# An attention and mixture-of-experts kernel on one core: embeddings loaded first, two more filler products, the first batch's W2 split moved into eight steps in a row

## The chip, the cores and the metric

One core of a Trainium2 chip (trn2) runs the whole program. Times are device microseconds (us) of one execution. The kernel before was timed in three runs.

## What is computed

A compressed attention turns its output into tokens; every token then goes to one of eight experts. Cut to what matters:

```python
# batch 8, heads 8, seq 576, head_dim 64, 32 memory slots
a = softmax(phi over seq)                      # 576 x 32 per head
k_m, v_m = a.T @ k, a.T @ v                    # 32 x 64 per head
attn = softmax(q @ k_m.T / 8) ; o = attn @ v_m # 576 x 64 per head
x = o as (4608 tokens, 512)                    # heads side by side
en = expert_emb / norm(expert_emb)
logits = x/norm(x) @ en.T / tau                # 4608 x 8
e = argmax(logits); gate = softmax(logits)[e]
out = gate * (relu(x @ w1[e]) @ w2[e])         # w1 512x1024, w2 1024x512
```

## The kernel before

Every engine runs its instructions in the order in which the program writes them; waits between engines and transfers are semaphores. Transfers start on three queues: SyncE's (SP), ScalarE's (ACT) and GpSimd's (POOL).

**The head.** The first batch's `phi` comes in two halves on SP's queue, then its keys and values in four tiles `kx0` to `kx3`, then `q`. ACT's queue carries the last 64 rows of keys and values (`kl`), the expert embeddings (`emb`, into part of `sT`) and `tau`. ACT takes the exponential of the first half of `phi` (`softmax`), then the square sum of the embeddings (`router`, the line with `AF.Square`), then the exponential of the second half. TensorE (PE) transposes the exponentials in three groups (`turn`, tiles `te`), with filler products on a constant between them (`warm`, tile `hot`), and multiplies them with the keys and values, tile by tile (`slots`, tiles `acc0t` and `acc0m`, the order of tiles is 0, 1, tail, 2, 3). The next batch's `phi`, keys and values are loaded behind these, and its transposes and `slots` run in the head as well.

**A batch.** `project` and `first` make h = relu(x W1) in 16 steps of six products (tile `ph`, four PSUM buffers in rotation). After each step ACT writes the rounded `hh` (and, from step 8 on, `h4`), and VectorE (DVE) the remainder `hl`; a buffer is free when both have read it. `second` multiplies by W2 (tile `py`, out of the same rotation): first the last 64 tokens, straight from `w2s`, then the others from the rounded `wh` and the remainder `wl`.

**The split of W2.** `split_w` makes `wh` and `wl` of one eighth of W2: a cast `wh<-w2s` (for the first batch on ACT, later on POOL) and a subtract `wl<-w2s,wh` on POOL.

**The steps.** `steps` hangs other work behind the steps of `first` and `second`. For the first batch, the norms and gates of its tokens (`late`, of `root`, `sqrt` and `gates`: small DVE instructions of 128x5 and 128x40 on SBUF tiles) are spread behind steps 3 to 8 of `first`; behind step 8 comes ACT's exponential `l` (in `gates`), which needs DVE's subtract in the line before it. Behind steps 9 and 11 stand the copies of the next batch's scores.

Of the kernel before, what the change touches and what calls it, by code (L numbers as in the profile page):

```python
# [21 lines left out]
N, DM, E, FF = B * S, H * D, 8, 1024  # L22
# [208 lines left out]
class Kernel:  # L231
# [60 lines left out]
    def consts(self):  # L292
# [9 lines left out]
        nc.vector.tensor_scalar(out=self.eb, in0=self.i8, scalar1=1.0 / (E * P), scalar2=None, op0=ALU.mult)  # L302
        nc.vector.memset(self.vv, 0.0)

    def load_router(self):
        nc, st = self.nc, self.st.tile
        self.em, self.hq = (self.sT[:E, 1, :DM], self.w2s[:E, 7])
        nc.scalar.dma_start(self.em, self.emb)
        self.tv = st([E, 1], F32, name="tv")
        nc.scalar.dma_start(self.tv, self.tau.broadcast_to((E, 1)))  # L310
        nc.scalar.activation(st([P, 1], F32, name="e8"), self.ones[:, :1], AF.Exp)
# [378 lines left out]
    def steps(self, b, t, u):  # L690


        first, second = ([[] for _ in range(n)] for n in (16, 40))

        for j in range(8):
            copy = self.nc.gpsimd.tensor_copy if b else None
            at = first[j if b else 9 + j * 2] if b or j < 4 else second[j - 4]
            at.append(lambda copy=copy: self.split_w(copy))
        if not b:
            late = t.late()  # L700
            first[2].append(lambda: t.attend(3, 4))
            first[3].append(lambda: t.norm(3, 4))
            first[4] += [t.total, lambda: self.load_kv(2)]

            for f in range(3, 9):
                first[f].append(lambda: next(late))
            first[12] += [lambda: self.keep(0), lambda: self.load_q(2)]
        if u:
            c, o = b + 1, 0 if b else 3
            if not b:  # L710
                first[9].append(lambda: self.scores(c))
            for k in range(2):
                first[(3 + k if b else 9 + 2 * k)].append(lambda k=k: self.results(c, k))

            places = (first[6], first[8], first[10], first[12]), (first[12], first[14], second[0], second[3])
            if not b:
                places = (second[3], second[3], second[3], second[7]), (second[7], second[7], second[7], second[10])
            all = slice(0, BL)
            for g in range(NG):
                work = u.weigh((g,), all)  # L720
                places[g][0].append(lambda g=g: u.fill((g,), all, [self.sT[:, i] for i in range(NG)]))
                for at in places[g][1:]:
                    at.append(lambda work=work: next(work, None))
            for at, g in zip((second[0], second[3]) if b else (second[7], second[10]), range(NG)):
                at.append(lambda g=g: (u.divide((g,), all), u.lay(g), u.turn((g,), all)))
            o = 0 if b else 7
            second[17 + o].append(lambda: u.attend(0, 1, pt=self.mm))
            second[19 + o].append(lambda: u.attend(2, 3))
            second[21 + o].append(lambda: u.attend(4))
            second[22 + o] += [lambda: self.load_w2(u.choose()), self.parts, lambda: self.keep(c)]  # L730
            second[23 + o] += [u.owner, u.flags]
            for n, i in enumerate(((0, 1), (2, 3), (4,)) if b else ((2, 3), (4,), (0, 1))):
                second[24 + n + o].append(lambda i=i: u.norm(*i))
            after = u.late()
            for n in (27, 28, 29, 30, 31, 32):
                second[n + o].append(lambda: next(after))
            second[32 + o].append(lambda: list(after))
            m = b + 2
            if m < B:
                for g in range(NG):  # L740
                    second[11 + 3 * g + o].append(lambda g=g: self.softmax(m, (g,)))
                second[18 + o].append(lambda: self.shares(m))
                second[(28 if b else 25) + o].append(lambda: [self.turn(m, i, min(i + 4, 9)) for i in (0, 4, 8)])
                at = second[(31 if b else 28) + o]
                at += [lambda: self.slots(m), lambda: self.blocks(m, 0), lambda: self.blocks(m, 1, True)]
                for g in range(NG):
                    second[(35 + 2 * g if b else 31 + g) + o].append(lambda g=g: self.flip(m, g))
        return first, second
# [152 lines left out]
@with_exitstack  # L901
def moe_linformer(ctx, tc, phiT, qT, kv, kvt, emb, tau, w1, w2, out):
    k = Kernel(ctx, tc, phiT, qT, kv, kvt, emb, tau, w1, w2, out)
    ctx.enter_context(tc.manual_schedule(engines={ET.PE, ET.DVE, ET.Activation, ET.SP, ET.Pool}))


    k.eights()
    k.warm(11)
    k.load_phi(0)
    k.load_kv(0)  # L910
    k.load_q(0)
    k.load_router()
    k.consts()
    accs = [k.ps.tile([P, 4, 2 * D], F32, tag=f"{n}3", name=f"acc0{n}", bufs=1) for n in "tm"]
    for acc in accs:
        k.nc.vector.memset(acc, 0.0)
    router = k.router()
    for g in range(NG):
        k.largest(0, g)
        k.softmax(0, (g,))  # L920
        next(router)
    for i in (0, 4, 8):
        k.turn(0, i, min(i + 4, 9))
        if i < 8:
            k.warm(2)
    k.shares(0)
    k.load_phi(1)
    t = Tokens(k, 0, k.pt)
    keys, values = slice(0, 1), slice(1, 2)
    for ks in ((0, 1), (4,), (2,), (3,)):  # L930
        k.slots(0, accs, ks=ks, first=0 in ks, last=3 in ks)
        if ks[0] < 3:
            k.warm(1)
    k.block(0, 0)
    k.load_kv(1)
    k.flip(0, 0, keys)
    k.block(0, 1, which=(0,))
    k.flip(0, 1, keys)
    first, others = slice(0, 4), slice(4, BL)
    ts = [k.mm([P, P], f"ts0_{g}", 1 + g) for g in range(NG)]  # L940
    k.score(0, ts, 0, P)
    t.fill(range(NG), first, ts)
    k.block(0, 1, which=(1,))
    next(router, None)
    k.flip(0, 0, values)
    k.flip(0, 1, values)
    ts = [k.mm([P, S - P], f"tr0_{g}", g) for g in range(NG)]
    k.score(0, ts, P, S)
    k.squares(0, [k.pt([P, D + E], f"tl0_{g}") for g in range(NG)])
    list(t.weigh(range(NG), first))  # L950
    k.products(0)
    k.warm(5, 2)
    t.divide(range(NG), first)
    t.turn(range(NG), first)
    k.largest(1, 0)
    k.softmax(1, (0,))
    t.attend(0, pt=lambda shape, name: k.mm(shape, name, 2), turned=False)
    e = t.choose((0,))
    k.largest(1, 1)
    k.softmax(1, (1,))  # L960
    k.load_q(1, (0,))
    t.turned(0)
    for i in (0, 4, 8):
        k.turn(1, i, min(i + 4, 9))
        k.turns += not i
        if not i:
            k.warm(8, hot=t.spare)
    t.fill(range(NG), others, ts)
    weights = [t.weigh((g,), others) for g in range(NG)]
    for g in range(NG):  # L970
        next(weights[g])
    for g in range(NG):
        next(weights[g])
        list(weights[g])
    t.owner()
    k.shares(1, v=k.nc.gpsimd)
    k.slots(1, accs)
    k.block(1, 0, alone=True)
    k.tags = 4
    for g in range(NG):  # L980
        k.part(g, slice(0, P), k.nc.scalar.copy)
    k.block(1, 1, alone=True)
    k.flip(1, 0)
    t.divide(range(NG), others)
    t.turn(range(NG), others)
    for g in range(NG):
        k.part(g, slice(P, HS), k.nc.scalar.copy)
    t.norm(0)
    k.load_q(1, (1,))
    k.load_w2(e)  # L990
    k.load_phi(2)
    k.warm(3)
    for b in range(B):
        u = Tokens(k, b + 1, k.pt) if b < B - 1 else None
        left = k.batch(b, t, u)
        t = u
    k.rest(*left)
# [29 lines left out]
```

## Time and profile before

| | before |
|---|---|
| median of 3 runs | 418.95 us (418.62 to 420.69) |
| profiled execution | 421.38 us |
| its span, first to last instruction | 419.0 us |
| PE busy | 97% of the span |
| DVE, ACT, POOL busy | 63%, 41%, 40% |
| mean granted PE clock | 0.992 |

The profiled execution is one execution with its own time, 2.4 us over its span and 2.4 us over the median of the timed runs. Stretches below are counted from the start of its span. "Line" is a line of the program; "released by" in brackets is what ended the idle time before an instruction.

### The profile page before, as it was taken

The page shows a single profiled execution, that of the slowest core. Times are in us where ns is not written, and L with a number is a line of the kernel's source. Part 1 is how long each engine was busy: PE and PEld are TensorE (multiplying, and loading weights), DVE is VectorE, ACT ScalarE, POOL GpSimd, SP SyncE. Part 2 cuts the span into 40 slices and gives each one's busy share as a digit, 9 for nine tenths or more (in the row PEclk, how much of TensorE's full clock was granted, in tenths as well). Part 3 has the DMA queues.
Part 4 walks back from the last instruction along what each step waited for, and adds up shares of the span by engine and source line. Part 5 has one row for each costly group of instructions (what it writes and reads, how often), then busy time and mean ns, then how long its engine had stood idle before and what let it go on. Part 6 is the DMA issues. An engine that isn't in the chain of part 4 may idle for free. (4 is left out here: it accounts for less than half of the span.)

```text
span 419.0 us, 9431 instructions
## 1 busy us (share of the span) xinstructions
PE 405.8 (97%) x3489; PEld 329.5 (79%) x3489; DVE 262.4 (63%) x839; ACT 173.2 (41%) x476; POOL 168.6 (40%) x196
## 2 busy tenths in 40 slices
PE   6989999999999999999999999999999999999993
PEld 2458878788877978879787988879788888879783
DVE  4597796679664795648772695648955495745000
ACT  4466742375225722356313642357223661145110
POOL 0032380387132942259130960339331681359000
PEclk9899999999999999999999999999999999999998
DMA  8979926896769824995469926798349404690101
GB/s 272 345 281 344 362 85 156 283 371 268 154 214 398 334 50 118 344 372 218 75 206 378 364 89 148 241 386 318 60 127 366 155 0 96 201 398 10 37 36 47
DMA packets 69858, 91.19 MB, mean 218 GB/s; under 512 B 41800, under 2 KB 47688, under 8 KB 69808
## 3 DMA queue, kind: packets, MB, share of 16 engines
q1 hardware_dynamic: 66928, 82.00, 59.3%
q0 software_dynamic: 2688, 8.26, 5.3%
q8 instruction: 29, 0.48, 0.5%
q10 hardware_dynamic: 192, 0.28, 0.3%
q14 instruction: 21, 0.17, 0.1%
HBM read 71.19 MB, written 19.33 MB: 216 GB/s over the span
## 5 line engine op out<-in xcount | busy, mean ns | idle before, releaser
L628 PE MATMUL ph<-aT,gh 128*128 128x288 f32 x512 | 103.2, 297 | 0.5 <-DVE gl L612 0.5
L681 PE MATMUL py<-wh,hh 128*128 128x512 f32 x248 | 102.3, 413 | 0.0
L681 PE MATMUL py<-wl,hh 128*128 128x512 f32 x248 | 97.0, 391 | 0.3 <-POOL wl L599 0.3
L681 PE MATMUL py<-wh,hl 128*128 128x512 f32 x248 | 97.1, 392 | 0.0
L599 POOL TENSOR_TENSOR wl<-w2s,wh 128x512 fp32r<-128x512 f32 x64 | 83.4, 1306 | 16.8 <-ACT wh L598 12.3
L628 PEld LDWEIGHTS ph<-aT,gh 128*128 128x128 f32 x512 | 81.7, 188 | 3.0 <-DVE gl L612 1.4
L628 PE MATMUL ph<-aT,gl 128*128 128x288 f32 x256 | 75.4, 294 | 0.0
L634 DVE SCALAR_TENSOR_TENSOR hl<-ph,hh 128x288 fp32r<-128x288 f32 x128 | 56.0, 449 | 22.6 <-ACT hh L631 16.6
L631 ACT ACTIVATE hh<-ph 128x288 fp32r<-128x288 f32 x128 | 52.4, 417 | 32.9 <-PE ph L628 32.3
L686 ACT ACTIVATE ys<-py,gate 128x512 f32<-128x512 f32 (+1 forms) x39 | 25.0, 641 | 96.0 <-issue 48.3
L789 POOL DMA_DIRECT2D out_dram<-ys x28 | 15.5, 553 | 118.2 <-ACT ys L686 110.5
L681 PEld LDWEIGHTS py<-wh,hh 128*128 128x128 f32 x248 | 46.6, 188 | 12.0 <-issue 3.9
L681 PEld LDWEIGHTS py<-wh,hl 128*128 128x128 f32 x248 | 46.5, 188 | 10.2
L681 PEld LDWEIGHTS py<-wl,hh 128*128 128x128 f32 x248 | 46.7, 188 | 8.5 <-POOL wl L599 0.7
L628 PEld LDWEIGHTS ph<-aT,gl 128*128 128x128 f32 x256 | 48.0, 188 | 0.0
L589 POOL TENSOR_TENSOR aT<-aw,aT 128x576 fp32r<-128x576 f32 (+3 forms) x20 | 24.5, 1240 | 43.9 <-PE py L681 33.8
L612 DVE TENSOR_TENSOR gl<-pg,gh 128x512 fp32r<-128x512 f32 x32 | 20.0, 683 | 34.9 <-ACT gh L611 34.9
L598 POOL CAST wh<-w2s 128x512 fp32r<-128x512 f32 x56 | 37.5, 669 | 0.6 <-DMA w2s<-w 0.6
L670 PE MATMUL py<-w2s,h 128*64 128x256 f32 x256 | 29.4, 382 | 0.0
L427 ACT ACTIVATE ex<-ex,nm 128x576 f32<-128x576 f32 x16 | 12.3, 770 | 30.9 <-DVE nm L412 29.9
L670 PEld LDWEIGHTS py<-w2s,h 128*64 128x64 f32 x256 | 17.7, 137 | 9.4 <-DVE hl L634 1.1
L119 DVE TENSOR_REDUCE lg<-po 128x8 f32<-128x16 f32 x40 | 6.8, 173 | 28.1 <-PE po L114 28.0
(168 smaller groups left out, 522.6 us busy)
## 6 DMA issues: line engine op xcount, KB each, us to landing
kx<-kv SPq DMA_DIRECT2D x32, 512.0 KB, 7.0
w2s<-w SPq DMA_DIRECT2D x32, 512.0 KB, 10.2
w1s<-w SPq DMA_DIRECT2D x28, 512.0 KB, 6.5
out_dram<-ys POOLq DMA_DIRECT2D x28, 256.0 KB, 6.0
qt<-qT SPq DMA_DIRECT2D x12, 576.0 KB, 8.4
ad<-aw SPq DMA_DIRECT2D x8, 576.0 KB, 13.0
td<-x SPq DMA_DIRECT2D x56, 72.0 KB, 2.2
ea<-td SPq DMA_DIRECT2D x7, 512.0 KB, 4.1
```

The source lines that it names most:

```text
L427: nc.scalar.activation(x, x, AF.Exp, bias=nm[:, g : g + 1], accum_out=sm[:, g : g + 1])
L589: self.nc.gpsimd.tensor_tensor(out=al, in0=a, in1=ah.bitcast(F32), op=ALU.subtract)
L598: (copy or self.nc.scalar.copy)(h, x)
L599: self.nc.gpsimd.tensor_tensor(out=l, in0=x, in1=h.bitcast(F32), op=ALU.subtract)
L612: nc.vector.tensor_tensor(out=self.gl[:, g, f], in0=ps[g], in1=self.gh[:, g, f].bitcast(F32), op=ALU.subtract)
L628: nc.tensor.matmul(p, lhsT=w[:, g, fs], rhs=x[:, g, to], start=g == 0 and k == 0, stop=g == 1 and k == 2)
L631: nc.scalar.activation(self.hh[:, f, to], p, AF.Relu)
L634: nc.vector.scalar_tensor_tensor(out=self.hl[:, f, to], in0=p, scalar=0.0, in1=self.hh[:, f, to].bitcast(F32), op0=ALU.max, op1=ALU.subtract)
L670: nc.tensor.matmul(p[64 * j : 64 * j + 64], lhsT=self.h4[:, f], rhs=self.w2s[:, f, d * j : d * j + d], start=f == 0, stop=f == 7,)
L681: nc.tensor.matmul(p, lhsT=h[:, f, to], rhs=w[:, f], start=f == 0 and k == 0, stop=f == 7 and k == 2)
L686: nc.scalar.activation(y[:, :d], p, AF.Copy, scale=gate[:, i : i + 1])
L789: eng.dma_start(self.out[r : r + P], y)
```

## The change

Three things change. The load of the embeddings becomes a function of its own and is called ahead of the load of `kl`, so it is first on ACT's queue. The filler products between the first two groups of transposes are four where they were two. The first batch's eight splits, which stood behind steps 9, 11, 13 and 15 of `first` and steps 0 to 3 of `second`, stand behind steps 6 to 13 of `first`, one for each.

```diff
+    def load_emb(self):
+        self.em, self.hq = (self.sT[:E, 1, :DM], self.w2s[:E, 7])
+        self.nc.scalar.dma_start(self.em, self.emb)
+
     def load_router(self):
         nc, st = self.nc, self.st.tile
-        self.em, self.hq = (self.sT[:E, 1, :DM], self.w2s[:E, 7])
-        nc.scalar.dma_start(self.em, self.emb)
...
         for j in range(8):
             copy = self.nc.gpsimd.tensor_copy if b else None
-            at = first[j if b else 9 + j * 2] if b or j < 4 else second[j - 4]
-            at.append(lambda copy=copy: self.split_w(copy))
+            first[j if b else 6 + j].append(lambda copy=copy: self.split_w(copy))
...
     k.load_phi(0)
+    k.load_emb()
     k.load_kv(0)
...
     for i in (0, 4, 8):
         k.turn(0, i, min(i + 4, 9))
         if i < 8:
-            k.warm(2)
+            k.warm(2 if i else 4)
```

ACT's order behind steps 6 to 9 of `first`, batch 0 (`ph_06`, `ph_07`, `ph_10` and `ph_11` are the steps 6 to 9; the line numbers after `_` only count tiles). Before:

```order
L631 ACTIVATE hh<-ph_06_660 128x288
L631 ACTIVATE hh<-ph_07_674 128x288
L631 ACTIVATE hh<-ph_10_687 128x288
L633 ACTIVATE h_96<-ph_10_687 128x64
L213 ACTIVATE l_683<-l_683 128x40
L631 ACTIVATE hh<-ph_11_706 128x288
L633 ACTIVATE h_96<-ph_11_706 128x64
L598 CAST wh<-w2s 128x512
```

and with the change:

```order
L633 ACTIVATE hh<-ph_06_662 128x288
L600 CAST wh<-w2s 128x512
L633 ACTIVATE hh<-ph_07_678 128x288
L600 CAST wh<-w2s 128x512
L633 ACTIVATE hh<-ph_10_693 128x288
L635 ACTIVATE h_96<-ph_10_693 128x64
L600 CAST wh<-w2s 128x512
L213 ACTIVATE l_689<-l_689 128x40
L633 ACTIVATE hh<-ph_11_714 128x288
L635 ACTIVATE h_96<-ph_11_714 128x64
L600 CAST wh<-w2s 128x512
```

Three casts stand ahead of the exponential `l` where there was none; the fourth stands where the first stood.

DVE's order in the same place is the same in both programs; so it reads with the change, from the remainder of step 5 to that of step 8:

```order
L636 SCALAR_TENSOR_TENSOR hl<-ph_05_650,hh 128x288
L42 RECIPROCAL nrr<-nrg 128x5
L43 SCALAR_TENSOR_TENSOR nrr<-nrr,ss_208 128x5
L44 SCALAR_TENSOR_TENSOR nrg<-nrg,nrr 128x5
L636 SCALAR_TENSOR_TENSOR hl<-ph_06_662,hh 128x288
L42 RECIPROCAL nrr<-nrg 128x5
L43 SCALAR_TENSOR_TENSOR nrr<-nrr,ss_208 128x5
L44 SCALAR_TENSOR_TENSOR n_618<-nrg,nrr 128x5
L196 TENSOR_SCALAR n_618<-n_618 128x5
L197 RECIPROCAL n_618<-n_618 128x5
L636 SCALAR_TENSOR_TENSOR hl<-ph_07_678,hh 128x288
L209 TENSOR_TENSOR m_209<-m_209,n_618 128x5
```

Nothing moved here; what moved is POOL's work beside it, since each subtract `wl` follows its cast.

## Rows read from the trace of the kernel before

**Rows 1.** The page's first part: busy us, share of the span, instructions.

```profile
PE 405.8 (97%) x3489; PEld 329.5 (79%) x3489; DVE 262.4 (63%) x839; ACT 173.2 (41%) x476; POOL 168.6 (40%) x196
```

**Rows 2.** Waits of PE over the whole span: us, times, longest.

```profile
PE te L449 <- ACT ex L427: 2.2, 1, 2.2
...
PE py L681 <- POOL wl L599: 0.3, 1, 0.3
```

**Rows 3.** Timeline of the head: start, us, engine, line, tiles, idle before and releaser.

```profile
6.00 0.75 DVE L412 TENSOR_REDUCE nm<-ex 128x1 f32<-128x576 f32 x1 [1.06 <-DMA ex<-phiT]
...
6.44 0.59 PE L351 MATMUL hot<-ones 128*128 128x512 bf16 x2
...
7.73 0.63 ACT L319 ACTIVATE w2s<-sT 8x512 f32<-8x512 f32 x1 [1.90 <-DMA sT<-emb]
...
8.36 0.76 ACT L427 ACTIVATE ex<-ex,nm 128x576 f32<-128x576 f32 x1
...
9.26 1.12 PE L449 MATMUL te<-ident,ex 128*128 128x128 f32 x4 [2.23 <-ACT ex L427]
...
14.54 0.43 PE L469 MATMUL acc0t<-kx,eT 128*32 128x128 f32 x8
```

**Rows 4.** Busy time by stretch; PEclk is the granted clock, then DMA share, GB/s.

```profile
11.00:12.00 1.00, 1.00 (x14) 0.59 (x16) 0.95 (x6) 0.27 (x2) 0.00 (x0) 0.50 1.13 338
```

**Rows 5.** SP's own timeline: the issue of the first batch's last tile, `kx3`.

```profile
5.28 0.61 SPq L375 DMA_DIRECT2D kx<-kv  x1
```

**Rows 6.** DMA issues of that moment and of ACT's `kl`: KB, us to landing.

```profile
kx<-kv SPq DMA_DIRECT2D x1, 512.0 KB, 6.7
...
kl<-kvt ACTq DMA_DIRECT2D x2, 128.0 KB, 4.9
```

**Rows 7.** Busy time by stretch as in Rows 4, from 20 to 25 us.

```profile
20.00:22.00 2.00, 1.04 (x7) 0.65 (x6) 1.84 (x7) 0.61 (x2) 0.00 (x0) 1.00 1.03 404
...
23.20:24.00 0.80, 0.80 (x6) 0.34 (x5) 0.80 (x3) 0.59 (x1) 0.00 (x0) 1.00 0.05 20
24.00:25.00 1.00, 1.00 (x6) 0.43 (x5) 1.00 (x3) 0.97 (x4) 0.49 (x3) 1.00 0.00 0
```

**Rows 8.** PE's timeline: the last 12 of 32 products of the next batch's `acc0t`.

```profile
26.00 0.51 PE L469 MATMUL acc0t<-kx,eT 128*32 128x128 f32 x12
```

**Rows 9.** DVE's timeline, 53 to 61 us.

```profile
53.74 1.72 DVE L72 TENSOR_TENSOR x<-x,mx 128x576 f32<-128x576 f32 x1
...
60.01 0.76 DVE L84 TENSOR_TENSOR x<-x,z 128x576 f32<-128x576 f32 x1
```

**Rows 10.** One line, POOL's subtract, 40 to 60 us: ns minimum, median, maximum.

```profile
L599 POOL TENSOR_TENSOR wl<-w2s,wh x8: 1285/1292/1826, 46.6 to 57.8; 128x512 fp32r<-128x512 f32 x8
```

**Rows 11.** Two lines of DVE over the whole span, columns as in Rows 10.

```profile
L193 DVE TENSOR_SCALAR ss<-ss x8: 172/427/435, 41.0 to 362.8; 128x5 f32<-128x5 f32 x8
...
L634 DVE SCALAR_TENSOR_TENSOR hl<-ph,hh x128: 410/456/459, 37.2 to 387.1; 128x288 fp32r<-128x288 f32 x128
```

**Rows 12.** Timeline of the first batch's steps 6 to 9.

```profile
41.96 0.41 ACT L631 ACTIVATE hh<-ph 128x288 fp32r<-128x288 f32 x1 [0.38 <-PE ph L628]
...
42.97 0.17 DVE L43 SCALAR_TENSOR_TENSOR nrr<-nrr,ss 128x5 f32<-128x5 f32 x1
...
43.83 0.17 DVE L43 SCALAR_TENSOR_TENSOR nrr<-nrr,ss 128x5 f32<-128x5 f32 x1
...
45.41 0.24 ACT L213 ACTIVATE l<-l 128x40 f32<-128x40 f32 x1 [1.33 <-DVE l L211]
...
45.95 0.62 ACT L598 CAST wh<-w2s 128x512 fp32r<-128x512 f32 x1
```

**Rows 13.** Timeline: the start of `second`, and the last eighth of W2 in it.

```profile
50.52 3.22 PEld L670 LDWEIGHTS py<-w2s,h 128*64 128x64 f32 x32 [0.18 <-DVE hl L634]
...
59.02 0.39 PE L681 MATMUL py<-wh,hh 128*128 128x512 f32 x1
...
59.70 0.50 PE L681 MATMUL py<-wl,hh 128*128 128x512 f32 x1 [0.29 <-POOL wl L599]
```

## The prediction

> **What bounds the kernel.** I read the page first: PE is busy for 97% of the span, the next engine for 63% [rows 1]. So I asked where PE is not at work, and read its waits: the longest single one, 2.2 us, is that of the second group of transposes for ACT's exponential, in the head, and the change's other place shows up too, 0.3 us for the last remainder of W2 [rows 2]. Both lie in the first 60 us, and no other PE wait is longer than about 1 us. From there on PE goes from product to product, so what the first 60 us win or lose stays in the time; that is my rule for every term below. I then read the timelines of the two places and, for each, what would be late next.
>
> **The load of the embeddings.** The chain in the head is: ACT's square sum waits 1.90 us for the embeddings and starts at 7.73; the exponential behind it in ACT's queue starts at 8.36, 0.63 later; the transposes start at 9.26, 0.90 after that [rows 3]. Moved to the front of ACT's queue, the embeddings (16 KB) take the place of `kl`, whose two loads of 128 KB took 4.9 us from issue to landing at about 0.7 and 1.3 us [rows 6]; a smaller load there should land by 5 us at the latest. ACT was idle for 1.90 before 7.73, so the square sum can start at 5.83 and the exponential at 6.46. It then waits for DVE's maximum of the second half, which ends at 6.75 [rows 3]: 6.79 instead of 8.36, and the transposes begin at 7.69 instead of 9.26, 1.57 earlier. `kl` is issued one load later, and is not wanted before about 13 us; that costs nothing.
>
> **The two more products.** They fill part of PE's wait. Before, the two fillers end at 7.03 and PE idles for 2.23 us; afterwards the granted clock is 0.50, the 1.2 GHz level, in the stretch from 11 to 12 us [rows 3, 4], and four transposes take 1.12 us. With the second group at 7.69, four fillers of 0.2 to 0.3 us from 6.44 end between 7.3 and 7.6, so PE stands still for less than 0.4 us. I take the clock to stay at the upper level. The products of `kx3`, which started at 14.54 [rows 3], would be ready at 12.97 at half clock (7.69, plus the 5.28 us between these two starts), and at least 1 us sooner at the upper level, an estimate from over 2 us of this work at half clock: by 12.0. But `kx3` itself is issued at 5.28 and lands 6.7 later, at 12.0 [rows 5, 6]. So they start at 12.0: 2.5 earlier. If the clock falls anyway, 1.6 is left; if `kx3` lands sooner and PE is ready sooner, perhaps 2.9.
>
> **What is late next in the head.** The same 2.5 passes to the next batch's products, whose last tile `kx3` begins in the last 8 of 32 products, at about 26.15 (12 are left at 26.00) [rows 8]; moved, at 23.65. Traffic of these tiles runs at a DMA share of 1.03 from 20 to 22, trickles on at 20 GB/s until 24.0 and stops [rows 7]. The DMA engines were busy here and in the stretch from 11 to 12 as well (1.13) [rows 4], so issuing the tiles earlier hardly moves their end. I take 24.05 for it: the head wins 2.1, between 1.6 (slow clock) and 2.5 (tile lands 0.4 sooner).
>
> **The split.** What it removes: in `second` PE waits for the last remainder; product to product is 0.23, here 0.68 (59.02 to 59.70) [rows 13], so 0.45 is won once POOL is done earlier. What it adds: between `l` and step 12 ACT's queue had two casts (behind steps 9 and 11) and has three (9, 10 and 11), ahead of `hh` and `h4` of step 12, whose PSUM buffer the first product of `second` takes; that product already waited for the remainder `hl` [rows 13], so one cast of 0.62 [rows 12] counts in full: 0.6. The first three casts fall into idle time of ACT, the 1.33 before `l` and the 0.38 after each step [rows 12]; they cost nothing there themselves.
>
> But each cast starts a subtract on POOL, 1.29 us long [rows 10], and the first three now run from about 43.0 (41.96, 0.3 to the next start, 0.62 for the cast) to 46.8, beside DVE's small instructions for norms and gates, where POOL was idle before. Does that matter? DVE's tensor_tensor of 128x576 takes 0.76 at 60.01, when POOL has finished, and 1.72 at 53.74 beside a subtract; and a tensor_scalar of 128x5 has a median of 0.427 beside POOL's subtracts against 0.172 in the first batch, where POOL is idle [rows 9, 11]. One of POOL's subtracts is lengthened to 1.83 by the same meeting [rows 10]. The remainders `hl`, which read PSUM, stay at 0.41 to 0.46 in all 128 places [rows 11]. So DVE instructions with SBUF operands only wait until the running subtract ends. L43, L44 and their like are such instructions. No row shows one of these two beside a subtract: each wait is between 0 and 1.29; I take the full one, as the nearest row, 53.74, has 0.96.
>
> The Trainium skill ("SBUF — State Buffer", section "Who interferes with whom") states this as a lock: a VectorE instruction with two SBUF inputs and a GpSimd instruction that reads SBUF exclude each other for a whole instruction. By that rule the wait is the full rest of the subtract, which gives the forecast below; where the wait is nothing for so small an instruction, it is rival 1's time.
>
> Walk it through. L43 at 42.97 [rows 12] meets the first subtract and ends with it at 44.25; L44 behind it meets the second, to 45.5; the next L43, due at 43.83, meets the third and ends at 46.75 instead of 44.0, 2.75 late. Then POOL runs dry: the fourth cast stands behind `l` in ACT's queue, and `l` waits for DVE. So DVE's chain, `l` (45.41 becomes 48.15) and all behind it on ACT, `hh` of step 9 among it, are 2.75 late; PE stalls at steps 10 to 13 for buffers, and `second` starts 2.75 + 0.6 = 3.35 late. Less 0.45, the split costs 2.9. Its lower end, no wait, is 0.6 - 0.45 = 0.15; its upper end, with a fourth meeting (the fourth subtract and the last gates), some 4.
>
> **Sum.** -2.1 + 2.9 = +0.8: the profiled execution would go from a span of 419.0 to 419.8. The profiled execution has 421.38 in all, 2.4 over the median; the term is added to the median: 418.95 + 0.8, about 419.7.
>
> **Rivals.**
> 1. *DVE does not wait* for such small instructions. For it: no row shows L43 beside a subtract. Against: 128x5 waited in L193. Then -2.1 + 0.15: 417.0; and where `kx3` of the next batch also lands in time, -2.5 + 0.15: 416.6.
> 2. *The head wins nothing.* Transfers are busy through the head; if the next batch's last tile landed no earlier than its products started before, 26.15, the waits of the split stand alone: 418.95 + 2.9 = 421.85. It decides, that is makes the kernel slower by over 0.5%, from a landing of about 25.3 on. Against: traffic ends at 24.0 [rows 7].
> 3. *The change doesn't do what it says*: the embeddings land late all the same, say at 7.0. Then the square sum starts at 7.0, the exponential at 7.63, the transposes at 8.53, and the products of `kx3` at 12.8 (5.28 later, less 1): 1.7 is won and the time is 420.15. Against: `kl`, sixteen times as large, landed in 4.9 us [rows 6]. It lies inside the forecast's own range.
>
> **How the numbers follow.** Forecast with rival 3: 0.68, time 419.7, its own range 418.5 to 420.9. Rival 1: 0.21, of which 0.12 at about 416.6 and 0.09 about 417.0. Rival 2: 0.11. A measurement of this kernel tells some 0.5%, 2.1 us, from no change: below 416.85 is faster, above 421.05 slower. So faster 0.12, same 0.77, slower 0.11. The range takes in the forecast, most of rival 1 and the near edge of rival 2: 416.6 to 421.2.
>
> **What would show it.** Right: ACT's square sum near 5.9 without a wait; transposes near 7.7; clock 1.00 from 9 to 12; PE's products of `kx3` near 12.0 and, for the next batch, a short wait near 24; in the first batch L43 and L44 of over 1 us beside POOL's subtract, `l` waiting over 2 us for DVE, PE waiting for `hl` at steps 10 to 13 and at the start of `second`, and no wait of `py` for `wl`. Wrong: L43 at 0.17 beside a subtract, or a head that moves by less than 1.5.

## The result, and the profile after

| | before | after |
|---|---|---|
| median, same chip | 420.69 us (418.62 to 420.99, 7 executions) | 423.17 us (422.38 to 423.93, 7 executions) |
| profiled execution | 421.38 us | 423.93 us |
| its span | 419.0 us | 422.1 us |

The ratio of the times is 1.0073, 95% interval 1.005 to 1.0096: slower, by some 3.1 us by that ratio and 2.5 between the two medians, where 419.7 and no change were forecast. 423.17 lies outside the range.

PE's share of the span is 96% where it was 97% [rows 1]. The page's first line of the kernel after:

```profile
PE 406.3 (96%) x3491; PEld 329.4 (78%) x3491; DVE 263.2 (62%) x839; ACT 172.8 (41%) x476; POOL 167.7 (40%) x196
```

PE's waits of the kernel after (us in total, times, longest), beside [rows 2]:

```profile
PE acc0t L471 <- DMA kx<-kv: 2.2, 2, 1.6
PE ph L630 <- DVE hl L636: 1.7, 3, 1.0
...
PE py L672 <- DVE hl L636: 0.5, 1, 0.5
```

Both old waits are gone, that of `te` for the exponential and that of `py` for the last `wl`. In their place PE waits for the key tiles in the head, and for DVE's remainder `hl` in steps 11, 13 and 14 (10 to 13 were forecast) and at the start of `second`. The second was forecast, the first was not. The head of the kernel after, as in [rows 3]:

```profile
5.28 0.61 ACT L321 ACTIVATE w2s<-sT 8x512 f32<-8x512 f32 x1
...
5.89 0.76 ACT L429 ACTIVATE ex<-ex,nm 128x576 f32<-128x576 f32 x1
...
6.85 0.61 PE L451 MATMUL te<-ident,ex 128*128 128x128 f32 x4
...
9.57 0.42 PE L471 MATMUL acc0t<-kx,eT 128*32 128x128 f32 x8 [1.57 <-DMA kx<-kv]
...
10.67 0.43 PE L471 MATMUL acc0t<-kx,eT 128*32 128x128 f32 x8 [0.68 <-DMA kx<-kv]
...
14.00 0.66 PE L471 MATMUL acc0t<-kx,eT 128*32 128x128 f32 x8
```

The square sum, the exponential and the transposes are even earlier than forecast (6.85 for 7.69, and 9.26 before). But `kx0` is not there when PE asks for it at 8.0, PE stands still to 9.57, and the products of `kx3` start at 14.00: 0.54 earlier than before, not 2.5. The busy table of the kernel after shows what lies behind both halves of this, with the columns of [rows 4]:

```profile
4.00:7.00 3.00, 2.92 (x15) 1.38 (x14) 1.93 (x8) 2.99 (x9) 0.19 (x1) 1.00 0.87 212
12.00:15.00 3.00, 3.00 (x49) 1.36 (x43) 0.27 (x1) 0.00 (x0) 0.00 (x0) 0.50 1.08 373
```

From 4 to 7 us the DMA engines are busy 0.87 and move 212 GB/s; in the kernel before it was 1.01 and 284. The granted clock is 0.50, the 1.2 GHz level, from 12 to 15 us, so it fell after all, behind the new wait. That is one execution, and not the usual one: its mean clock of 0.991 is the lowest of the seven, and the median one had 0.996. Among the DMA issues up to 9 us (columns of [rows 6]) the four tiles take 8.5 us to their landing, and took 6.6 in the same stretch before:

```profile
kx<-kv SPq DMA_DIRECT2D x4, 512.0 KB, 8.5
```

The first batch's steps 6 to 9 of the kernel after, as in [rows 12], and the first `x<-x,mx` of [rows 9]:

```profile
42.70 3.81 POOL L601 TENSOR_TENSOR wl<-w2s,wh 128x512 fp32r<-128x512 f32 x3 [6.82 <-ACT wh L600]
...
42.90 1.15 DVE L44 SCALAR_TENSOR_TENSOR nrg<-nrg,nrr 128x5 f32<-128x5 f32 x1
...
44.55 0.74 DVE L43 SCALAR_TENSOR_TENSOR nrr<-nrr,ss 128x5 f32<-128x5 f32 x1
...
45.33 1.20 DVE L44 SCALAR_TENSOR_TENSOR n<-nrg,nrr 128x5 f32<-128x5 f32 x1
...
47.73 0.24 ACT L213 ACTIVATE l<-l 128x40 f32<-128x40 f32 x1 [3.37 <-DVE l L211]
...
57.08 0.76 DVE L72 TENSOR_TENSOR x<-x,mx 128x576 f32<-128x576 f32 x1
```

Three of DVE's instructions that take 0.17 elsewhere take 1.15, 0.74 and 1.20 beside POOL's three subtracts: 2.58 more in sum. `l` starts at 47.73 instead of 45.41. What that does to PE is read from the first product of `first` to the first of `second`, in the kernel before and then in the kernel after:

```profile
34.48 0.53 PE L628 MATMUL ph<-aT,gh 128*128 128x288 f32 x2
...
50.52 3.67 PE L670 MATMUL py<-w2s,h 128*64 128x256 f32 x32
```

```profile
34.22 0.53 PE L630 MATMUL ph<-aT,gh 128*128 128x288 f32 x2
...
53.35 3.67 PE L672 MATMUL py<-w2s,h 128*64 128x256 f32 x32 [0.47 <-DVE hl L636]
```

It takes 16.04 us before and 19.13 after, 3.09 more; the forecast was 3.35.

### The profile page after: what moved, and what is told of

Same layout as the page of the kernel before. It is cut to its first block, busy times and chain, and to the rows that moved or that the text cites. A ratio compares the mean times of both kernels' runs of the same rounds, so it can differ in the third digit from the quotient of the medians.

```text
span 422.1 us, 9435 instructions
## 1 busy us (share of the span) xinstructions
PE 406.3 (96%) x3491; PEld 329.4 (78%) x3491; DVE 263.2 (62%) x839; ACT 172.8 (41%) x476; POOL 167.7 (40%) x196
## 5 line engine op out<-in xcount | busy, mean ns | idle before, releaser
L601 POOL TENSOR_TENSOR wl<-w2s,wh 128x512 fp32r<-128x512 f32 x64 | 82.5, 1291 | 14.5 <-ACT wh L600 10.0
```

Of the source, the lines that this page charges most:

```text
L601: self.nc.gpsimd.tensor_tensor(out=l, in0=x, in1=h.bitcast(F32), op=ALU.subtract)
```

## The experiments

Each run has the times of 12 executions, one of them profiled (the split alone has 6, the kernel before again only the profiled one). Kernels of one group below shared a chip and the runs of the kernel before.

**First group: the two parts apart, and the split without its meeting.** Split alone:

```diff
-            at = first[j if b else 9 + j * 2] if b or j < 4 else second[j - 4]
-            at.append(lambda copy=copy: self.split_w(copy))
+            first[j if b else 6 + j].append(lambda copy=copy: self.split_w(copy))
```

> Only the split of W2 is moved to steps 6 to 13; the head is that of the kernel before. Theory (DVE's small SBUF instructions wait behind POOL's subtracts): L44, L43 and L44 take 0.7 to 1.3 us each beside the first three subtracts, the exponential l waits for DVE about 2.4 us later than before, second starts about 3 us later, py's wait for wl is gone; the time is 2.2 to 2.9 us above before. Rival (the loss comes from the head or from the two together): within 1 us of before.

Head alone (the new `load_emb`, called ahead of `load_kv(0)`, and the fillers; the split as before):

```diff
+    k.load_emb()
     k.load_kv(0)
...
-            k.warm(2)
+            k.warm(2 if i else 4)
```

> Only the head is changed: embeddings first, four filler products; the split as before. Theory (the key tiles land over 1 us later and take the gain away): the second transposes near 6.9, PE waits for the first key tiles until 9 to 10.7, and the first batch starts 0 to 0.6 us earlier: the time is 0 to 0.6 us below before. Rival (the late key tiles were chance of one execution, and the 2.1 us of the forecast are there): 1.8 to 2.5 us below before.

The whole change, with POOL's first three subtracts held behind the gates; their casts stay at steps 6 to 8:

```diff
+    def rests(self):
+        pool = self.nc.gpsimd
+        pool.tensor_copy(out=self.st.tile([P, 1], F32, name="gd"), in_=self.gate[:, 0, :1])
+        for j in range(3):
+            x, h, l = self.w2s[:, j], self.wh[:, j], self.wl[:, j]
+            pool.tensor_tensor(out=l, in0=x, in1=h.bitcast(F32), op=ALU.subtract)
...
+            if not b and j < 3:
+                first[6 + j].append(lambda j=j: self.nc.scalar.copy(self.wh[:, j], self.w2s[:, j]))
+                continue
...
+            first[8].append(self.rests)
```

> The changed kernel, but POOL starts the first three subtracts only when the gates are done (a copy of one gate column on POOL is ahead of them); the casts on ACT stay at steps 6 to 13. Theory (DVE behind POOL): L43 and L44 are at 0.17 again, l waits for DVE no longer than before, second starts only 0.4 to 0.6 us later than before, and the time is 2.2 to 3.0 us below the changed kernel, so 0 to 0.8 us below before. Rival (eight casts in a row crowd ACT's queue): the time stays with the changed kernel, 2 us or more above before.

The whole change, with the eight splits in a row from step 9:

```diff
-            first[j if b else 6 + j].append(lambda copy=copy: self.split_w(copy))
+            at = first[j if b else 9 + j] if b or j < 7 else second[0]
+            at.append(lambda copy=copy: self.split_w(copy))
```

> The changed kernel with the eight splits in a row from step 9 on (9 to 15 of first and step 0 of second), behind the last of the small DVE instructions of the norms. Theory (DVE behind POOL): no L43 or L44 over 0.2 us; one or two more casts ahead of step 12 delay second by 0.6 to 1.1 us, the wait for wl is gone or short: 1.5 to 2.5 us below the changed kernel. Rival (a row of splits costs by itself, wherever it starts): within 0.7 us of the changed kernel.

| | median us | to before (419.46) |
|---|---|---|
| split alone | 423.83 (421.44 to 424.88) | 1.0092 [1.0065, 1.012] |
| head alone | 420.27 (419.34 to 421.35) | 1.0004 [0.9986, 1.0021] |
| subtracts late | 420.51 (419.18 to 422.24) | 1.0024 [1.0007, 1.0041] |
| split from step 9 | 420.12 (419.33 to 422.06) | 1.0014 [0.9996, 1.0031] |

The split costs all of the loss, and the head gives nothing. The split alone lies 4.4 us over the median of before, where 2.2 to 2.9 were forecast: four of its six executions had a mean clock of 0.991 to 0.994, and the two at 0.997 took 421.44 and 421.68, about 2.4 over the 419.16 that the executions of before with 0.995 or more have on this chip. The head alone (0.8 over before, where 0 to 0.6 below was forecast) and the late subtracts (1.1 over, where 0 to 0.8 below was forecast) missed as well; part of that is the program's end, further down. Take the subtracts away from DVE's norms and gates, in either of two ways, and 2.7 to 3.1 us of the 423.17 are gone (over two groups of runs), or 2.1 to 2.5 by the ratios to each group's own kernel before. From the first product of `first` to that of `second`, a stretch behind the head, it is 19.31 us with the split alone, 16.04 with the head alone, 16.54 with the subtracts late and 16.55 with the split from step 9. The timeline of the late subtracts shows DVE and POOL apart:

```profile
43.79 0.17 DVE L43 SCALAR_TENSOR_TENSOR nrr<-nrr,ss 128x5 f32<-128x5 f32 x1
43.99 0.17 DVE L44 SCALAR_TENSOR_TENSOR n<-nrg,nrr 128x5 f32<-128x5 f32 x1
...
46.98 3.78 POOL L609 TENSOR_TENSOR wl<-w2s,wh 128x512 fp32r<-128x512 f32 x3
```

Eight casts in a row on ACT stand in this run as in the change. So the row of casts is not what costs.

With the head alone, PE waited for the tiles again (PE's waits, and the issues up to 9 us):

```profile
PE acc0t L471 <- DMA kx<-kv: 0.8, 2, 0.6
```

```profile
kx<-kv SPq DMA_DIRECT2D x4, 512.0 KB, 8.0
```

The row leaves out the longest wait, 1.30 us before the products of `kx0` at 9.30, which is put down to a DVE instruction that ended just then. But the clock stayed at the upper level, and the products of `kx3` started at 12.96, 1.6 earlier than in the profile of before. That a head 1.6 us earlier gave no time was the riddle. The 29 executions of the kernel before on this chip answer it in part: 19 had a mean granted clock of 0.995 to 0.997 and took 418.57 to 419.82, ten had 0.992 to 0.994 and took 420.34 to 421.68. The profile on which the prediction rests (421.38, clock 0.992) was one of the dear ones. So the next group profiled the kernel before once more.

**Second group: the clock, and why the tiles are late.** The kernel before, unchanged:

> The kernel before, profiled once more, nothing changed. Its 29 timed executions fall into two groups: 19 with a mean granted clock of 0.995 to 0.997 at 418.6 to 419.8 us, 10 with 0.992 to 0.994 at 420.3 to 421.7. Theory: the groups differ by the half-clock stretch in the head (9 to 13 us), and the profile on which the prediction rests was of the dearer group (421.38). Then this profile, if its mean clock is 0.995 or more, has no 0.50 between 9 and 13, the first batch's kx3 products near 12.4 instead of 14.54, and a time near 419.1; if its clock is 0.992 to 0.994, it repeats the first one. Rival: the two groups come from somewhere else (the program's end, a later stage); then the head looks the same at either time.

Only the two more fillers:

```diff
-            k.warm(2)
+            k.warm(2 if i else 4)
```

> The kernel before with only the two more fillers (four between the first two groups of transposes). Theory: the half-clock stretch in the head comes where PE stands still for long before the second transposes (2.23 us in the first profile of before, 1.43 in the split-only run, which kept its clock); 0.6 us more of fillers removes it, all executions fall into the cheaper group, median 418.9 to 419.2, none over 420.3. Rival: the fillers don't touch the clock; a third of the executions stay at 420.3 to 421.7 and the median at 419.4 to 419.7.

Head alone, with `kx2` and `kx3` held back:

```diff
-            for k in range(4):
+            for k in range(4 if b else 2):
                 self.nc.sync.dma_start(self.kx[k], self.kv[b, :, k])
+
+    def load_held(self):
+        self.nc.gpsimd.tensor_copy(self.kx[2][:, 0, :1], self.e(0, 1)[:, :1])
+        for k in (2, 3):
+            self.nc.sync.dma_start(self.kx[k], self.kv[0, :, k])
...
+    k.load_held()
+    k.load_q(0)
```

> The head's part of the change alone, and the tiles kx2 and kx3 held on SP's queue until the second half of phi has landed (a one-element copy on POOL writes into kx2), so that kx2 is issued near 4.9 us as before instead of 2.7. Theory A: the tiles land 1.2 us late because all four are under way together; then kx0 lands near 8.2 again (9.2 in head-only), kx3 near 12.0 (12.9), its products start by 12.2 and the median is 419.0 to 419.5. Theory B: the tiles land late because kl, issued behind the embeddings, now shares the DMA engines with them; then kx0 stays near 9.2, kx3 near 12.9 or later, and the median stays near 420.3 or above.

Head alone, with `kl` behind the tiles:

```diff
+            for k in range(0 if b else 4):
+                self.nc.sync.dma_start(self.kx[k], self.kv[b, :, k])
...
-                (self.nc.sync if b else self.nc.scalar).dma_start(to, x)
-            for k in range(4):
+                self.nc.sync.dma_start(to, x)
+            for k in range(4 if b else 0):
...
-    for ks in ((0, 1), (4,), (2,), (3,)):
+    for ks in ((0, 1), (2,), (3,), (4,)):
```

> The head's part of the change alone, and kl taken from ACT's queue and loaded on SP behind kx3 (its products after those of kx3), so that no kl traffic stands beside the tiles until they are all issued. Theory B (late kl slows the tiles): kx0 lands by 8.2, kx3 by 12.0, median 418.8 to 419.5. Theory A (four tiles under way together): the tiles are issued as close together as in head-only, kx0 stays near 9.2, median near 420.3. In both q is issued later by the two loads, about 0.6 us, which the scores at 14 us may feel.

| | median us | to before (419.68) |
|---|---|---|
| before again | 419.33 (one execution), clock 0.996 | |
| fillers alone | 419.93 (419.53 to 421.70) | 1.0 [0.9979, 1.0022] |
| tiles held | 420.57 (419.63 to 421.37) | 1.0013 [0.9994, 1.0032] |
| tail last | 420.29 (418.46 to 422.26) | 1.0018 [0.9997, 1.0039] |

One stretch of the first profile of the kernel before, with the columns of [rows 4]:

```profile
10.00:13.00 3.00, 3.00 (x38) 1.83 (x36) 2.01 (x12) 0.85 (x2) 0.00 (x0) 0.57 1.06 363
```

The kernel before, profiled again; the timeline has the columns of [rows 3]:

```profile
9.00:10.00 1.00, 0.91 (x6) 0.72 (x7) 0.80 (x6) 0.72 (x3) 0.24 (x1) 1.00 1.04 418
10.00:13.00 3.00, 3.00 (x76) 1.73 (x78) 1.88 (x11) 0.59 (x2) 0.00 (x0) 1.00 1.05 359
```

```profile
9.09 0.66 PE L449 MATMUL te<-ident,ex 128*128 128x128 f32 x4 [1.94 <-ACT ex L427]
...
12.83 0.43 PE L469 MATMUL acc0t<-kx,eT 128*32 128x128 f32 x8
```

The transposes start as in [rows 3], 0.17 earlier, but the clock is 1.00 throughout and the products of `kx3` start at 12.83, not 14.54: 1.71 earlier, and the span is 1.7 shorter. So the half-clock stretch of [rows 4] belongs to some executions only, and they are some 2 us longer. (There is one profile of each kind; of the other executions only the mean clock is known.) It also solves the riddle: against 12.83 the head alone, at 12.96, is not earlier at all. Over the four groups the kernel before ran 104 times: 59 executions with a mean clock of 0.995 or more have a median of 419.16, 45 with 0.994 or less one of 421.0.

Tiles held: theory A falls. SP issued `kx2` and `kx3` at 4.60, near their old time, and PE still waited 1.09 and 0.76 for `kx0` and `kx1` (SP's own timeline, then PE's):

```profile
4.60 1.10 SPq L382 DMA_DIRECT2D kx<-kv  x2
```

```profile
9.43 0.43 PE L476 MATMUL acc0t<-kx,eT 128*32 128x128 f32 x8 [1.09 <-DMA kx<-kv]
10.62 0.43 PE L476 MATMUL acc0t<-kx,eT 128*32 128x128 f32 x8 [0.76 <-DMA kx<-kv]
```

Tail last: with no `kl` beside the tiles, the products of `kx0`, `kx1` and `kx3` start at 7.88, 8.68 and 11.75, as theory B wants:

```profile
7.88 0.42 PE L473 MATMUL acc0t<-kx,eT 128*32 128x128 f32 x8
8.68 0.43 PE L473 MATMUL acc0t<-kx,eT 128*32 128x128 f32 x8 [0.37 <-DMA kx<-kv]
...
11.75 0.42 PE L473 MATMUL acc0t<-kx,eT 128*32 128x128 f32 x8 [0.85 <-DMA kx<-kv]
```

Its median is no better. The products of `kl` now come last, from 12.65 on (in the kernel before, profiled again, the last are those of `kx3`, from 12.83 on), and five of its twelve executions had a mean clock of 0.989 or 0.990 and took 421.2 to 422.3 (its profiled one took 418.46). So it tells where the tiles' time went, and is no better kernel.

The fillers alone did what they were to do: one of twelve executions was over 420.7, where ten of 29 of the kernel before were. But the other eleven took 419.5 to 420.6, not 418.9 to 419.2. DVE's last instruction tells why. Fillers alone:

```profile
410.64 0.48 DVE L659 TENSOR_SCALAR ys<-py,gate 128x256 f32<-128x256 f32 x1 [24.63 <-PEq L811]
```

It ends at 411.12 and the span at 418.1: 7.0 later. In the kernel before, profiled again, it starts at 410.78 and the span ends 6.0 behind it. The work was 0.14 us shorter and the program's end 0.9 longer. What lies outside the span took some of it back: 1.8 us, where the kernel before has 1.9 to 2.8 and mostly 2.2 to 2.4. Every version with more than two fillers has 1.8 or 1.9 there; why is open.

**Third group: the program's end, and the embeddings on another queue.** The kernel before with five fillers:

```diff
-            k.warm(2)
+            k.warm(2 if i else 5)
```

> The kernel before with five fillers between the first two groups of transposes, one more than in the fillers-only run. That run ended its last DVE instruction at 410.64 us of a span of 418.1, 7.0 us ahead of its end; the kernel before, profiled again, at 410.78 of 417.3, 6.0 ahead. Theory: the 0.9 us more at the program's end hang on the number of TensorE's instructions (2249 before, 2253 with four fillers, 2255 in the tail-last run, which had 5.0), by where the last ones lie in TensorE's code; with five fillers there are 2255, so the last DVE instruction ends 5 to 6 us ahead of the span's end, executions lie at 418.6 to 419.3 and the median is near 419.0. Rival: the end varies by chance or with the fillers' work; then it stays near 7.0 and the median near 419.9. In both nearly all executions keep a mean clock of 0.994 or more, and none of the dearer group of before (420.3 to 421.7) is left.

The same, and the embeddings first on POOL's queue:

```diff
+    def load_emb(self):
+        self.em, self.hq = (self.sT[:E, 1, :DM], self.w2s[:E, 7])
+        self.nc.gpsimd.dma_start(self.em, self.emb)
...
+    k.load_emb()
     k.load_kv(0)
```

> As the five fillers, and the embeddings loaded first on POOL's queue, so that kl stays first on ACT's. Theory C: the tiles land 1.0 to 1.2 us late in the head's change because kl, put behind the embeddings, no longer runs beside phi; then with kl in its old place no packet of kx takes 0.8 us or more before 7 us, kx0 lands near 8.2 and kx3 near 12.0, its products start by 12.3, and the median is 418.4 to 419.0. Rival D: an early start of the exponentials and the square sum, whatever the queue, makes the tiles late; then kx0 lands near 9.2 and kx3 near 13, its products start near 13, and the median is 419.3 or more.

Five fillers: 418.62 (418.33 to 419.27), to before (419.10) 0.9985 [0.997, 1.0]. Embeddings on POOL's queue: 417.90 (417.69 to 418.76), 0.996 [0.9938, 0.9983]. With five fillers DVE's last instruction ends 6.0 us ahead of the span's end (417.2):

```profile
410.69 0.48 DVE L659 TENSOR_SCALAR ys<-py,gate 128x256 f32<-128x256 f32 x1 [24.66 <-PEq L811]
```

One filler more, and 1.3 us less, of which some 0.3 may be the chip (the kernel before with a mean clock of 0.995 or more has 418.82 here and 419.16 there). The end of the program goes with the number of TensorE's instructions, as the theory said, and no execution is left among the dear ones. (The tail-last run, which the expectation gives 5.0, had 5.5.) With `kl` first on ACT's queue and the embeddings on POOL's, the tiles are in time (timeline, then the issues up to 9 us):

```profile
7.26 0.76 ACT L429 ACTIVATE ex<-ex,nm 128x576 f32<-128x576 f32 x1
...
8.17 0.66 PE L451 MATMUL te<-ident,ex 128*128 128x128 f32 x4 [0.33 <-ACT ex L429]
...
11.91 0.43 PE L471 MATMUL acc0t<-kx,eT 128*32 128x128 f32 x8
```

```profile
kx<-kv SPq DMA_DIRECT2D x4, 512.0 KB, 6.9
```

The tiles take 6.9 us, not 8.0, PE does not wait for them, and the products of `kx3` start at 11.91. PE's one wait for a key tile comes later, for the last tile of the next batch:

```profile
23.99 0.42 PE L471 MATMUL acc0t<-kx,eT 128*32 128x128 f32 x8 [0.21 <-DMA kx<-kv]
```

The prediction had that tile land at 24.05. Theory C's times came true, and the median is 0.5 below its range. Rival D could live on this run alone, since the exponential starts at 7.26 here and at 5.89 in the change. The tail-last run settles it: there the exponential starts earlier still, and the tiles were in time.

```profile
5.74 0.76 ACT L431 ACTIVATE ex<-ex,nm 128x576 f32<-128x576 f32 x1
```

**Fourth group: the split on that head.** At steps 6 to 13, and in a row from step 9 (the diffs of the first group):

> The kernel with five fillers and the embeddings on POOL's queue (median 417.90), and the change's split at steps 6 to 13. Its head keeps the clock and its tiles are in time, so what is added is the split alone. Theory: three of DVE's small instructions wait behind POOL's subtracts, 2.1 to 2.8 us in all, one more cast stands ahead of step 12 (0.6) and the wait for wl goes (0.45): 2.3 to 2.9 us more, 420.2 to 420.8. Rival: most of the split's price in the earlier runs was the clock's or the program end's; then it adds under 1.2 us, 417.9 to 419.1.

> The same, with the eight splits in a row from step 9 on (seven in the steps 9 to 15 of the first product, one behind step 0 of the second). Theory: the meeting with DVE's norms and gates is gone, as in the run with the head's change, where step 9 showed L43 and L44 at 0.17 throughout; one more cast (0.6) and the wait for wl (0.45) nearly cancel, so 417.7 to 418.3. Rival: casts of eight steps in a row crowd ACT, whatever DVE does; then over 419.

Steps 6 to 13: 420.88 (420.19 to 421.93), 1.0006 [0.9986, 1.0025] to a kernel before of 420.78 on this chip. From step 9: 417.81 (417.75 to 419.04), 0.9943 [0.9925, 0.9961]. The same eight splits, three steps apart, differ by 3.07 us. POOL and DVE at steps 6 to 13:

```profile
41.51 3.77 POOL L601 TENSOR_TENSOR wl<-w2s,wh 128x512 fp32r<-128x512 f32 x3 [6.80 <-ACT wh L600]
...
41.52 1.31 DVE L43 SCALAR_TENSOR_TENSOR nrr<-nrr,ss 128x5 f32<-128x5 f32 x1
...
42.86 1.21 DVE L44 SCALAR_TENSOR_TENSOR nrg<-nrg,nrr 128x5 f32<-128x5 f32 x1
...
44.56 0.73 DVE L43 SCALAR_TENSOR_TENSOR nrr<-nrr,ss 128x5 f32<-128x5 f32 x1
```

and from step 9, where POOL's first subtract begins behind the last of them:

```profile
41.43 0.17 DVE L43 SCALAR_TENSOR_TENSOR nrr<-nrr,ss 128x5 f32<-128x5 f32 x1
41.63 0.17 DVE L44 SCALAR_TENSOR_TENSOR n<-nrg,nrr 128x5 f32<-128x5 f32 x1
...
44.24 1.30 POOL L601 TENSOR_TENSOR wl<-w2s,wh 128x512 fp32r<-128x512 f32 x1 [10.49 <-ACT wh L600]
```

From the first product of `first` to that of `second` it is 19.30 us at steps 6 to 13, 16.55 from step 9, and 16.02 with the split as before. The profile at steps 6 to 13 is the slowest of its twelve executions, and in it PE also waited 0.81 us for `q`. The version from step 9 and the one with the split as before are the best of the study; the 0.09 us between them, from two groups, tell nothing.

## Why the prediction was wrong

The step that failed is the head's term, 2.1 us of gain. It failed in two places, and a cost that it did not have came on top.

**The clock.** The sum took the 14.54 at which the products of `kx3` started in the profile, half clock and all, and added the difference to the median. "The profiled execution has 421.38 in all, 2.4 over the median" was written down and not asked about. 1.7 of these 2.4 us were the half-clock stretch, by the two profiles of the kernel before (14.54 and 12.83; spans of 419.0 and 417.3), and the median of 418.95 is that of an execution without it, by its time. In profiles without it the products of `kx3` start at 12.83 (before again), 12.44 (split alone) or 12.67 (five fillers). Against 12.0, where the prediction put them, there was 0.4 to 0.8 us to win, not 2.5. Embeddings on POOL's queue, which do reach 11.91, won 0.72 (418.62 to 417.90). "I take the clock to stay at the upper level" held in the profile of the head alone and failed in that of the change; but 59 of the 104 executions of the kernel before had nothing of the clock to win.

**The tiles.** "`kx3` itself is issued at 5.28 and lands 6.7 later, at 12.0" and "`kl` is issued one load later, and is not wanted before about 13 us; that costs nothing" took the transfers for unmoved. With the embeddings ahead of `kl` on ACT's queue they moved: in all five such runs the four tiles took 8.0 to 8.5 us (6.3 to 7.0 with the old head), and PE stood still 1.5 to 2.3 us before the products of the first two. It is the order on that queue that does it: embeddings on another queue, 6.9 to 7.2; tiles issued at their old times, still 8.3; `kl` off ACT's queue and behind the tiles, 6.9, with the exponential as early as in the change. How it does is not settled. In each of the five the DMA engines were less busy from 4 to 7 us (0.75 to 0.88, at 194 to 246 GB/s) than in the kernel before (1.01 and 0.97, 284 and 274) and with the embeddings on POOL's queue (0.96 to 1.00, 255 to 294). But with `kl` behind the tiles it was 0.87 and 239 GB/s too, and there the tiles were in time.

What the head's term said of the next batch was right: with the embeddings on POOL's queue its last tile is waited for until 23.99, and 24.05 was forecast. Rival 3 falls, since the square sum started at 5.28 without a wait.

**The program's end.** Two more products cost nothing where they stand, in PE's wait. With them the program's end is 0.9 us longer and the time 0.8 (419.16, the kernel before with a mean clock of 0.995 or more, to 419.93).

**The split**, 2.9 us, was right, mechanism and size. Three of DVE's small instructions each waited out POOL's subtract, 2.58 where 2.75 was forecast (2.74 on the clean head); `second` started 3.09 to 3.3 later, where 3.35 was forecast; PE waited for `hl` at steps 11, 13 and 14 (and 10, with the split alone and on the clean head) and at `second`; `py` no longer waited for `wl`. On a clean head the split cost 2.98 (417.90 to 420.88, on two chips, whose kernels before differ by 0.4 at a mean clock of 0.995 or more). The rule of the Trainium skill ("SBUF — State Buffer", section "Who interferes with whom"), that such a VectorE instruction and GpSimd's subtract exclude each other for a whole instruction, holds for an instruction of 128x5: 1.31 us beside a subtract of 1.26 (3.77 for three), 0.17 without. The +0.6 and -0.45 of one more cast and of `wl` cancel: from step 9, where they stand alone, `second` starts 0.53 later and the median moves by -0.09. Rival 1 (DVE does not wait) falls.

**The account.** From the kernel before with a mean clock of 0.995 or more, 419.16: the fillers with the program's end +0.77 (419.93), the embeddings with the late tiles +0.34 (420.27), the split +2.90 (423.17). These are differences of medians from three groups of runs on different chips; the ratios' intervals are about 0.2% to either side, some 0.8 us, so the small terms are no more than likely. The time lies on the far side of rival 2 ("the head wins nothing", 421.85), but that rival had the next batch's tile late; it was the first batch's, and the rival did not say that the half-clock stretch was missing from the median.

## What to carry to other kernels

Before a gain is read from a profile, ask whether its execution is like the median: one that is 2 us longer may hold a stretch that the median execution does not have, and taking that away wins nothing there. A load that goes to the front of a queue pushes another load back, and here the transfers beside that one moved too; a queue of its own for the small urgent load avoided it. Keep GpSimd's long two-operand work away from chains of small VectorE instructions, and look for the first step behind the chain: three steps later the same work was free.

## What the runs showed of the hardware

Four fillers instead of two made the program's end 0.9 us longer (7.0 for 6.0 us from DVE's last instruction to the span's end), and five brought it back to 6.0. With 3489 and 3492 matrix products on the page the end was short (5.4 to 6.0 us in eight profiles), with 3491 long (6.6 to 7.4 in six). Why is open; that it has to do with where TensorE's code lies, as the expectation of the five fillers supposed, was not shown.

The granted clock in the head falls in some executions and not in others of one kernel: before, PE stood still 2.23 us and the clock fell, and 1.94 us and it did not. With four or five fillers on the old head, executions as dear as those that had it were one of 12 and none of 12. But in the profiles of the change and of the late subtracts it fell behind the wait for the tiles (0.50 from 12 to 15 us, 0.60 from 10 to 13), and in that of the head alone, which stood still 1.30 and 0.56 us there, it did not.
